# Attention in front of a two-layer feed-forward: exponentials and values of two batches as float16 pairs, and weight loads planned behind the splits of q and k

## The chip, the cores and the metric

The kernel runs on one core of a Trainium2 chip. The metric is the device time of one execution in microseconds. The engines are called TensorE (PE in the rows, its weight loads PEld), VectorE (DVE), ScalarE (ACT), GpSimd (POOL) and SyncE (SP, which issues nearly all DMAs).

## The reference

`q`, `k`, `v` have 4 batches, 12 heads, 448 positions and 64 columns a head. The output of attention, with its heads side by side, is the input of the feed-forward layers (768 to 2048 to 768).

```python
scores = scale * np.matmul(q, k.transpose(0, 1, 3, 2))
scores = cap * np.tanh(scores / cap)
scores = scores - np.max(scores, axis=-1, keepdims=True)
attn = np.exp(scores)
attn = attn / (np.sum(attn, axis=-1, keepdims=True) + 1e-09)
x = np.matmul(attn, v)                 # then heads side by side: (1792, 768)
h = x @ w_in
g = np.where(h >= 1, h, np.where(h <= -1, 0.0, (h + 1) ** 2 / 4))
out = g @ w_out
```

## The kernel before

**Numbers.** Float32 operands of the large products are split into two float16 halves ("high" and "low"), and a product is three float16 matmuls: high by high, high by low, low by high. This is so for q by k, x by `w_in` and g by `w_out`. The one large product left in float32 is exponentials by v (`av`).

**Attention.** It works on pairs of heads: `n` = 0 to 23, six to a batch (`NPR`). For each `n`, `split` makes the halves of q and k (`spl`); then for each of four chunks of keys `c` (the last one holds half a chunk of each head), `qk` writes scores into one of two PSUM tiles `s`, `expo` runs tanh and exp on ScalarE into `e` (a ring of five), `add` sums exponentials on VectorE, and `av` multiplies `e` by `v` into the one PSUM bank `av`. The two heads of `av` go to the two halves of the array's columns. `norm` sums over partitions (`t`), takes a reciprocal on VectorE, spreads it back over the partitions with a small matmul (`mix` by `sel`), scales, and splits the result into the halves `x`, of which a ring of ten is kept.

**Feed-forward.** For each batch `b`, `h_mm` makes 16 blocks of h (`f` = x by w, 18 matmuls each, lines L431 to L433; they need all six `x` of the batch), `h_out` makes the halves of g from them, and `o_mm` makes 6 blocks of the output (48 matmuls each, L460 to L462). During batch 0 the weights are loaded and converted piece by piece (`piece`: 16 pieces of `w_in`, 12 of `w_out`, lines L252 to L258); the pieces land in seven slots, the six tiles of `w2` and `raw`. Batches 1 to 3 load weights, then q, k and v again for range checks (`piece_check`, `qkv_check`), and `x_check` checks every `x`; `verdict` decides at the end whether a general version of the kernel has to run.

**Order.** Nothing is issued in the order in which it is written. Every step is recorded in a `Plan` with a cost per engine and its dependences by buffer names. `Plan.order` runs a list scheduler backwards and forwards five times and keeps the order with the earliest planned end. That order is then written out; each engine, and SP's queue of DMAs too, works through its own list in that order. Steps of attention of batch `b + 1` may be placed beside the feed-forward of batch `b`. A dependence that is only in the plan moves things in the lists; on the chip an instruction waits for real overlaps of tiles alone.

Of the kernel before, what the change touches and what calls it, by code (L numbers as in the profile page):

```python
# [32 lines left out]
CV, CX, CG = (CQ + i * B * NPR for i in (1, 2, 3))  # L33
NCHK = CG + B
# [5 lines left out]
WS, XS, GS, QS = 2.0 ** 15, 2.0 ** 13, 4.0, 2.0 ** 10  # L40
# [19 lines left out]
RATE = 250  # L60
# [5 lines left out]
class Plan:  # L66
# [4 lines left out]
    def __init__(self):  # L71
        self.steps, self.buffers = [], {}

    def add(self, options, reads=(), writes=(), size=0):

        i, deps = len(self.steps), set()
        for keys, write in ((reads, False), (writes, True)):
            for buf, part in keys:
                parts = self.buffers.setdefault(buf, {})
                for p in list(parts) if part is None else (part, None):  # L80
                    if p in parts:
                        deps.add(parts[p][0])
                        if write:
                            deps |= parts[p][1]
# [9 lines left out]
        self.steps.append(({e: (c, f) for e, c, f in options}, deps, size))  # L94
# [71 lines left out]
def fast_body(ctx, tc, flag, qkp, vp, cap, w_in, w_out, out):  # L166
# [25 lines left out]
    es = ring("e", 5, [P, 2, S])  # L192
    sums = ring("sums", 2, [P, 2, S])
    xs = ring("x", 10, [P, 2, S], F16)
# [6 lines left out]
    ots = ring("ot", 2, [P, S])  # L201
# [33 lines left out]
    def piece(i):  # L235
# [16 lines left out]
        dma(8 * P * width, lambda: M.dma_start(t, src.bitcast(I32)), [], rk)  # L252
# [18 lines left out]
    def x_check(n):  # L271
        x, k = st["x", n]
        j = CX + n
        dve(S, lambda: V.tensor_reduce(out=chk[:, j:j + 1], in_=x[:, 0], op=ALU.max, axis=AX.X, apply_absolute_value=True), [(k, 0)], [("chk", j)])
# [31 lines left out]
    def load_qk(n):  # L306
        t, k = st["qkr", n] = take("qkr", qkr)
        dma(4 * P * (S + KP), lambda: M.dma_start(t, qkp[n]), [], k)
# [4 lines left out]

    def split(n):

        (raw, rk), (t, k) = st["qkr", n], take("spl", spl)
        hk, lk = [(k[0][0], 0)], [(k[0][0], 1)]
        either(rk, hk, act_(S + KP, lambda: A.activation(t[:, 0], raw, AF.Copy, scale=QS)), dve_(S + KP, lambda: V.tensor_scalar(t[:, 0], raw, scalar1=QS, scalar2=None, op0=ALU.mult), True))
        dve(S + KP, lambda: V.scalar_tensor_tensor(out=t[:, 1], in0=raw, scalar=QS, in1=t[:, 0], op0=ALU.mult, op1=ALU.subtract), rk + hk, lk)
        st["spl", n] = t, hk + lk  # L320

    def qk(n, c):
# [10 lines left out]
        pe(640, run, k, sk)  # L333

    def expo(n, c):
        (s, sk), (e, ek) = st["s", n, c], take("e", es)
        st["e", n, c] = e, ek
        w = 2 if c < 3 else 1
        act(w * S + 60, lambda: A.activation(e[:, :w], s[:, :w, :S], AF.Tanh, scale=tsc), sk + [("tsc", None)], ek)  # L339
        act(w * S + 110, lambda: A.activation(e[:, :w], e[:, :w], AF.Exp, scale=capb), ek + [("tsc", None)], ek)  # L340
# [17 lines left out]
    def av(n, c):  # L358
        if c == 0:
            st["av", n] = take("av", avs)  # L360
        (a, ak), (vt, vk), (e, ek) = st["av", n], st["vt", n], st["e", n, c]

        def run():
            for j in range(2):
                h = slice(j * D, (j + 1) * D)
                w, m = (vt[:, j * 3 + c], e[:, j]) if c < 3 else (vt[h, 6], e[h, 0])
                T.matmul(a[h, :S], lhsT=w, rhs=m, start=(c == 0), stop=(c == 3))  # L367
        pe(790, run, ek + vk + (ak if c else []), ak)

    def norm(n):  # L370
# [16 lines left out]
        dve(1400, lambda: V.reciprocal(rr, t[:, :S // 2]), tk, rk)  # L387
# [15 lines left out]
        dve(S, lambda: V.scalar_tensor_tensor(out=xf, in0=xf, scalar=XS, in1=t[:, :S], op0=ALU.mult, op1=ALU.mult), tk + fk, fk)  # L403
# [3 lines left out]
    def attention(n):  # L407

        split(n)
        if n + 2 < B * NPR:  # L410
            load_qk(n + 2)
        for c in range(NCK):
# [3 lines left out]
            av(n, c)  # L416
# [53 lines left out]

    load_qk(0)
    dma(4 * P, lambda: M.dma_start(capr, cap.partition_broadcast(P)), [], [("tsc", None)])
# [11 lines left out]
    act(1, lambda: A.activation(half, ones[:, :1], AF.Copy, scale=0.5 * math.sqrt(GS)), [("ones", None)], [("half", None)])  # L484
    dve(1, lambda: V.reciprocal(tsc, capr), [("tsc", None)], [("tsc", None)])
# [13 lines left out]
    for b in range(B):  # L499
        for fc in range(NFC):  # L500
# [28 lines left out]
def general_body(ctx, tc, qkt, v, vf, cap, w_in, w_out, out):  # L529
# [421 lines left out]
    with tc.manual_schedule():  # L951
        for options, _, _ in plan.steps:
# [36 lines left out]
```

## Time and profile before

| | |
|---|---|
| Three runs, median | 651.07 us (650.08 to 651.25) |
| The profiled execution | 651.0 us, span 649.2 us |
| TensorE busy | 625.9 us, 96% of the span |
| VectorE busy | 449.2 us, 69% |
| ScalarE busy | 358.1 us, 55% |
| Mean granted TensorE clock | 0.987 |

The span runs from the first to the last instruction on the core, and 1.8 us of the execution lie around it. The busy share of TensorE is the union of its matmuls' durations; matmuls overlap, so what a stream of matmuls costs is read from the distance between their starts.

### The profile page before, as it was taken

To read this page: it belongs to the slowest core of one execution; us is meant where nothing else is said; L and a number is where in the kernel's file an instruction comes from. 1 tells how busy PE (TensorE), PEld (TensorE's weight loads), DVE (VectorE), ACT (ScalarE), POOL (GpSimd) and SP (SyncE) were. 2 spreads that over 40 slices of the span, in tenths; PEclk is the share of its full clock that TensorE was granted. 3 is DMA by queue.
4 is the path that set the end of the run, shared out by engine and by line. 5 is a ranking of instruction groups with operands and counts; after the bars stand their busy time and mean duration, and the time that the engine had idled before them with its cause. 6 is when DMAs were issued, how large, how long until landed. Compare 5 with 4: busy or idle time off the path is not lost.

```text
span 649.2 us, 8777 instructions
## 1 busy us (share of the span) xinstructions
PE 625.9 (96%) x3541; PEld 280.4 (43%) x3541; DVE 449.2 (69%) x610; ACT 358.1 (55%) x525; POOL 0.9 (0%) x5
## 2 busy tenths in 40 slices
PE   7599899999999999999999999999999999999996
PEld 2123245433355555333345554433345554555553
DVE  6989999999999235799962215999771226988400
ACT  6588986799941145999910026989830005552000
POOL 0000000000000000000000000000000000000000
PEclk9969999999999999999999999999999999999998
DMA  8935424534346012333544321332314445778401
GB/s 310 348 115 192 152 85 172 175 126 137 106 163 205 29 63 98 128 109 123 173 151 146 129 78 54 137 94 64 113 65 159 131 151 163 258 247 258 144 29 33
DMA packets 25538, 91.11 MB, mean 140 GB/s; under 512 B 2960, under 2 KB 12176, under 8 KB 22416
## 3 DMA queue, kind: packets, MB, share of 16 engines
q1 hardware_dynamic: 25488, 90.45, 41.6%
q8 instruction: 30, 0.49, 0.3%
q14 instruction: 20, 0.16, 0.1%
HBM read 84.94 MB, written 5.51 MB: 139 GB/s over the span
## 4 chain that ended last, share of the span: by engine, by line
PE 87%; ACT 9%; DVE 2%; DMA 1%; issue 1%; SPq 0%; ACTq 0%
PE f L460 11%; PE f L462 11%; PE f L461 11%; PE f L431 11%; PE f L433 11%; PE f L432 11%; PE av L367 10%; PE s L332 7%; ACT e L339 3%; ACT e L340 3%; PE t L381 2%; DMA capr<-cap 1%; PE t L398 1%; PE t L385 1%; ACT w L257 0%
## 5 line engine op out<-in xcount | busy, mean ns | idle before, releaser
L431 PE MATMUL f<-x,w 128*128 128x448 f16 x384 | 135.6, 353 | 0.9 <-ACT ot L467 0.7
L460 PE MATMUL f<-g,w 128*128 128x448 f16 x384 | 135.5, 353 | 0.0
L432 PE MATMUL f<-x,w 128*128 128x448 f16 x384 | 135.3, 352 | 0.0
L462 PE MATMUL f<-g,w 128*128 128x448 f16 x384 | 135.3, 352 | 0.0
L433 PE MATMUL f<-x,w 128*128 128x448 f16 x384 | 135.3, 352 | 0.0
L461 PE MATMUL f<-g,w 128*128 128x448 f16 x384 | 135.3, 352 | 0.0
L467 ACT ACTIVATE ot<-f 128x448 f32<-128x448 f32 x24 | 13.0, 543 | 164.7 <-PE f L462 164.7
L269 DVE TENSOR_REDUCE chk<-raw 128x1 f32<-128x768 f32 (+1 forms) x56 | 58.2, 1059 | 63.2 <-DMA raw<-w_out 63.2
L367 PE MATMUL av<-e,vt 128*64 128x448 f32 (+1 forms) x384 | 90.7, 565 | 3.3 <-ACT e L340 2.6
L340 ACT ACTIVATE e<-e,capb 128x896 f32<-128x896 f32 x96 | 91.0, 949 | 2.8
L339 ACT ACTIVATE e<-s,tsc 128x896 f32<-128x896 f32 x96 | 86.5, 902 | 9.0 <-PE s L332 5.8
L332 PE MATMUL s<-spl 64*128 64x448 f16 (+1 forms) x504 | 72.7, 368 | 7.2 <-ACT e L339 4.1
L443 ACT ACTIVATE r<-f,half 128x448 f32<-128x448 f32 x64 | 40.1, 627 | 44.1 <-PE f L433 43.9
L431 PEld LDWEIGHTS <-w 128*128 128x128 f16 x384 | 37.5, 98 | 42.3 <-issue 9.5
L445 DVE SCALAR_TENSOR_TENSOR wr<-f,r 128x448 f32<-128x448 f32 x64 | 39.5, 617 | 22.0 <-ACT r L444 21.5
L460 PEld LDWEIGHTS <-w 128*128 128x128 f16 x384 | 37.5, 98 | 39.1 <-issue 5.0
L433 PEld LDWEIGHTS <-w 128*128 128x128 f16 x384 | 37.6, 98 | 35.1
L462 PEld LDWEIGHTS <-w 128*128 128x128 f16 x384 | 37.6, 98 | 35.1
L461 PEld LDWEIGHTS <-w 128*128 128x128 f16 x384 | 37.6, 98 | 34.1
L432 PEld LDWEIGHTS <-w 128*128 128x128 f16 x384 | 37.6, 98 | 33.5 <-issue 1.4
L332 PEld LDWEIGHTS <-spl 64*128 64x128 f16 (+1 forms) x504 | 23.1, 97 | 64.0 <-issue 48.9
L448 ACT ACTIVATE g<-wr 128x448 f16<-128x448 f32 x59 | 33.8, 574 | 29.5 <-DVE wr L445 29.2
(64 smaller groups left out, 576.2 us busy)
## 6 DMA issues: line engine op xcount, KB each, us to landing
qkr<-qkp SPq DMA_DIRECT2D x48, 480.0 KB, 3.9
raw<-w_out SPq DMA_DIRECT2D x17, 1024.0 KB, 5.1
raw<-w_in SPq DMA_DIRECT2D x18, 768.0 KB, 4.2
w<-w_in SPq DMA_DIRECT2D x14, 768.0 KB, 8.7
vt<-vp SPq DMA_DIRECT2D x48, 224.0 KB, 3.4
w<-w_out SPq DMA_DIRECT2D x7, 1024.0 KB, 5.1
out<-ot SPq DMA_DIRECT2D x24, 224.0 KB, 2.0
capr<-cap SPq DMA_DIRECT2D x1, 0.5 KB, 6.4
```

Source lines behind the costliest of these rows:

```text
L269: dve(width, lambda j=j, op=op: V.tensor_reduce(out=chk[:, j:j + 1], in_=hi, op=op, axis=AX.X, apply_absolute_value=True), rk, [("chk", j)])
L332: T.matmul(s[:, j, :S], lhsT=t[h, a, S + c * P:S + (c + 1) * P], rhs=t[h, b, :S], start=(i == 0), stop=(i == 2))
L339: act(w * S + 60, lambda: A.activation(e[:, :w], s[:, :w, :S], AF.Tanh, scale=tsc), sk + [("tsc", None)], ek)
L340: act(w * S + 110, lambda: A.activation(e[:, :w], e[:, :w], AF.Exp, scale=capb), ek + [("tsc", None)], ek)
L367: T.matmul(a[h, :S], lhsT=w, rhs=m, start=(c == 0), stop=(c == 3))
L431: T.matmul(ph, lhsT=w1[:, 0, fc, c], rhs=x[c][0][:, 0], start=(c == 0), stop=False)
L432: T.matmul(ph, lhsT=w1[:, 1, fc, c], rhs=x[c][0][:, 0], start=False, stop=False)
L433: T.matmul(ph, lhsT=w1[:, 0, fc, c], rhs=x[c][0][:, 1], start=False, stop=(c == NCC - 1))
L443: act(S + (170 if acc else 0), lambda: A.activation(r, ph, AF.Relu, bias=half, scale=0.5 * root / (WS * XS), **acc), fk + [("half", None)] ...
L460: T.matmul(po, lhsT=hi[:, fc], rhs=gv[:, 0], start=(fc == 0), stop=False)
L461: T.matmul(po, lhsT=lo[:, fc], rhs=gv[:, 0], start=False, stop=False)
L462: T.matmul(po, lhsT=hi[:, fc], rhs=gv[:, 1], start=False, stop=(fc == NFC - 1))
```

## The change

- In batches 2 and 3 (`n >= HALVED`, 12 pairs of heads) exponentials and v are split into float16 halves (`halve`, `halve_v`), and `av` becomes three float16 products; exp gets a bias `lnes`, which scales it by 32. The reciprocals of these batches are checked (two reductions per `n` in `norm`).
- `av` of batches 1 to 3 is recorded for two chunks at once, so that its matmuls stand together in TensorE's list.
- `x_check` looks at one `x` of each batch (4 in all) where it looked at every one (24).
- The load of `cap` goes to ScalarE's queue as its first instruction; the first load of q and k is cut in two, and so is its split. In the plan, the first six weight pieces depend on the splits of q and k (`gate`).
- The planner counts DMAs at 400 bytes per ns (`RATE`, was 250), and steps of attention of batches 2 and 3 get a lead of 30 us in its priorities (`AHEAD`).
- Buffers: `x` has 7 tiles (10 before), `ot` one (2 before); halves of e use the two `z` tiles of the weight conversion and one more.

```diff
-RATE = 250
+RATE = 400
+
+AHEAD = 30000.0
...
-            out, _, end = self.run(deps, users, [-t for t in late], WINDOW, True)
+            out, _, end = self.run(deps, users, [-t - s[3] for t, s in zip(late, self.steps)], WINDOW, True)
...
+    ehs = [t.bitcast(F16)[:, :4 * S].rearrange("p (a j s) -> p a j s", a=2, j=2) for t in zs] + ring("eh", 1, [P, 2, 2, S], F16)
+    vhs = ring("vh", 2, [P, 2, TC, D], F16)
-    xs = ring("x", 10, [P, 2, S], F16)
+    xs = ring("x", 7, [P, 2, S], F16)
-    ots = ring("ot", 2, [P, S])
+    ots = ring("ot", 1, [P, S])
...
-        dma(8 * P * width, lambda: M.dma_start(t, src.bitcast(I32)), [], rk)
+        gate = [("gate", i)] if i < NPR else []
+        dma(8 * P * width, lambda: M.dma_start(t, src.bitcast(I32)), gate, rk)
...
+    def cuts(n):
+        return (slice(0, S + 2 * P), slice(S + 2 * P, S + KP)) if n == 0 else (slice(0, S + KP),)
...
+            dve(m, lambda w=w: V.scalar_tensor_tensor(out=t[:, 1, w], in0=raw[:, w], scalar=QS, in1=t[:, 0, w], op0=ALU.mult, op1=ALU.subtract), rz + hk, lk + [("gate", n)])
...
+    def halve(n, c):
+        (e, ek), w = st["e", n, c], 2 if c < 3 else 1
+        i = turn["eh"] = (turn.get("eh", -1) + 1) % len(ehs)
+        t, k = ehs[i], ehk[i]
+        hk, lk = [(k, 0)], [(k, 1)]
+        either(ek, [(k, None)], act_(w * S, lambda: A.copy(t[:, 0, :w], e[:, :w])), dve_(w * S, lambda: V.tensor_copy(t[:, 0, :w], e[:, :w]), True))
+        dve(w * S, lambda: V.tensor_tensor(out=t[:, 1, :w], in0=e[:, :w], in1=t[:, 0, :w], op=ALU.subtract), ek + [(k, None)], lk)
...
-    def av(n, c):
+    def av(n, cs):
+        if n >= HALVED:
+            vh, vk = st["vh", n]
+            def run():
+                for c in cs:
+                    e = st["eh", n, c][0]
+                    for x, y in ((0, 0), (0, 1), (1, 0)):
+                        for j in range(2):
+                            h = slice(j * D, (j + 1) * D)
+                            w, m = (vh[:, x, j * 3 + c], e[:, y, j]) if c < 3 else (vh[h, x, 6], e[h, y, 0])
+                            T.matmul(a[h, :S], lhsT=w, rhs=m, start=(c == x == y == 0), stop=(c == 3 and x == 1))
+            pe(105 + 570 * len(cs), run, [k for c in cs for k in st["eh", n, c][1]] + vk + (ak if cs[0] else []), ak)
+            return
...
+        if n >= HALVED:
+            for j, op in ((CS + n - HALVED, ALU.max), (CS + B * NPR + n - 2 * HALVED, ALU.min)):
+                dve(S // 2, lambda j=j, op=op: V.tensor_reduce(out=chk[:, j:j + 1], in_=rr, op=op, axis=AX.X), rk, [("chk", j)])
...
-            av(n, c)
+            if n >= HALVED:
+                halve(n, c)
+            if n < NPR:
+                av(n, [c])
+            elif c % 2:
+                av(n, [c - 1, c])
...
+    plan.add([("ACT", 50, lambda: A.dma_start(capr, cap.partition_broadcast(P)))], [], [("tsc", None)], 4 * P)
     load_qk(0)
-    dma(4 * P, lambda: M.dma_start(capr, cap.partition_broadcast(P)), [], [("tsc", None)])
...
-                for n in range(NPR):
-                    x_check(b * NPR + n)
+                x_check(b)
...
             for n in range(NPR):
+                plan.lead = AHEAD * (b > 0)
                 attention((b + 1) * NPR + n)
+                plan.lead = 0.0
```

The lists move in many places; three are shown. The first is SP's list at the start of the program, before: the loads of the first two pairs (`qkr`), of `cap`, of v (`vt`) and of weight pieces (`w2_0` to `w2_5`), up to the load of the third pair.

```order
L308 DMA qkr0_87<-qkp 128x960
L308 DMA qkr1_88<-qkp 128x960
L472 DMA capr_67<-cap 128x1
L252 DMA w2_0_78<-w_in 128x1536
L312 DMA vt0_91<-vp 128x448
L252 DMA w2_1_79<-w_in 128x1536
L312 DMA vt1_92<-vp 128x448
L252 DMA w2_2_80<-w_in 128x1536
L252 DMA w2_3_81<-w_in 128x1536
L252 DMA w2_4_82<-w_in 128x1536
L252 DMA w2_5_83<-w_in 128x1536
L308 DMA qkr0_87<-qkp 128x960
```

And the same list now:

```order
L322 DMA qkr0_87<-qkp 128x704
L322 DMA qkr0_87<-qkp 128x256
L322 DMA qkr1_88<-qkp 128x960
L326 DMA vt0_91<-vp 128x448
L326 DMA vt1_92<-vp 128x448
L264 DMA raw_84<-w_in 128x1536
L322 DMA qkr0_87<-qkp 128x960
L264 DMA w2_0_78<-w_in 128x1536
L322 DMA qkr1_88<-qkp 128x960
L264 DMA w2_1_79<-w_in 128x1536
```

The third pair's load stood behind six weight pieces and stands behind one now; the fourth stands behind two, and `cap` has left this list.

The second place is VectorE's list at the start of the program; before (`x9` is the zeroed tile that 13 warm-up matmuls of TensorE read, L481):

```order
L488 MEMSET sel_71 128x256
L483 MEMSET ones_70 128x32
L489 MEMSET low_72 128x1
L477 MEMSET x9_109 128x224
L493 MEMSET sel_71 2x64
```

And now (`x6` is that tile; the reciprocal reads `capr`, which the DMA of `cap` writes):

```order
L551 MEMSET sel_71 128x256
L547 MEMSET lnes_101 128x1
L545 MEMSET ones_70 128x32
L548 RECIPROCAL tsc_68<-capr_67 128x1
L552 MEMSET low_72 128x1
L539 MEMSET x6_110 128x224
L549 TENSOR_SCALAR tsc_68<-tsc_68 128x1
```

The reciprocal of `cap` stood ten rows behind the memset of that tile and stands two rows ahead of it now.

The third place is TensorE's list at the first chunk of `n` = 12, before (the float32 product of both heads is one row):

```order
L433 LDWEIGHTS w1_77
L433 MATMUL f0_139<-x8_108,w1_77 128x448
L367 MATMUL av0_141<-e3_96,vt0_91 64x448 x2
L332 LDWEIGHTS spl1_90
L332 MATMUL s0_137<-spl1_90 128x448
```

And now, with six such pairs of rows for each chunk (`z0` and `z1` hold the halves of e):

```order
L524 MATMUL f1_140<-g2_113,w2_5_83 128x448
L408 LDWEIGHTS vh0_99
L408 MATMUL av0_141<-z0_85,vh0_99 64x448
...
L408 LDWEIGHTS vh0_99
L408 MATMUL av0_141<-z1_86,vh0_99 64x448
L522 LDWEIGHTS w2_5_83
L522 MATMUL f1_140<-g3_114,w2_5_83 128x448
```

Two chunks now stand together between output blocks of batch 0 (L522 to L524); before, the first chunk stood alone among blocks of h of batch 1 (L433).

## Rows read from the trace of the kernel before

**Rows 1.** The page's first line.

```profile
span 649.2 us, 8777 instructions
```

**Rows 2.** Busy time of each engine by stretch, then granted clock, DMA share, GB/s.

```profile
20.00:30.00 10.00, 5.52 (x36) 1.78 (x36) 9.80 (x14) 5.20 (x10) 0.00 (x0) 1.00 0.87 339
30.00:40.00 10.00, 6.70 (x29) 2.27 (x31) 9.99 (x14) 6.81 (x9) 0.00 (x0) 0.55 0.78 241
...
120.00:180.00 60.00, 60.00 (x400) 21.68 (x399) 57.86 (x69) 57.64 (x81) 0.00 (x0) 1.00 0.47 157
...
325.00:400.00 75.00, 75.00 (x398) 38.58 (x397) 27.25 (x33) 13.10 (x25) 0.00 (x0) 1.00 0.36 120
```

**Rows 3.** Timeline of the start: start, duration, engine, instruction, idle time before it.

```profile
1.46 5.04 PE L481 MATMUL f<-x 128*128 128x448 f16 x13 [1.46 <-DVE x L477]
...
6.43 1.59 PE L332 MATMUL s<-spl 64*128 64x448 f16 x12
8.10 0.16 DVE L485 RECIPROCAL tsc<-capr 128x1 f32<-128x1 f32 x1 [1.50 <-DMA capr<-cap]
...
8.55 1.01 ACT L339 ACTIVATE e<-s,tsc 128x896 f32<-128x896 f32 x1 [1.70 <-DVE tsc L486]
...
13.10 1.08 DVE L348 TENSOR_TENSOR sums<-e,e 128x896 f32<-128x896 f32 x1
```

**Rows 4.** Timeline from the third pair's load to the last x of batch 0.

```profile
10.10 0.33 SPq L308 DMA_DIRECT2D qkr<-qkp  x1
...
30.09 0.65 DVE L318 TENSOR_SCALAR spl<-qkr 128x960 f16<-128x960 f32 x1
30.66 0.61 DVE L405 TENSOR_TENSOR x<-xf,x 128x448 f16<-128x448 f32 x1
...
33.36 1.01 ACT L339 ACTIVATE e<-s,tsc 128x896 f32<-128x896 f32 x1 [3.06 <-PE s L332]
...
77.49 0.48 PE L398 MATMUL t<-mix,sel 128*128 128x224 f32 x2 [0.49 <-DVE mix L394]
...
80.96 0.61 DVE L405 TENSOR_TENSOR x<-xf,x 128x448 f16<-128x448 f32 x1
```

**Rows 5.** Landing of the q and k loads, from the view of that tile.

```profile
DMA to landing us min/median/max: 3.0/3.9/12.3
```

**Rows 6.** The page's DMA issues: KB each, median us to landing.

```profile
out<-ot SPq DMA_DIRECT2D x24, 224.0 KB, 2.0
```

**Rows 7.** Groups by line: busy us, mean ns of one, then idle time before.

```profile
L340 ACT ACTIVATE e<-e,capb 128x896 f32<-128x896 f32 x96 | 91.0, 949 | 2.8
...
L339 ACT ACTIVATE e<-s,tsc 128x896 f32<-128x896 f32 x96 | 86.5, 902 | 9.0 <-PE s L332 5.8 <-DVE tsc L486 1.7 <-PE av L367 1.4
...
L387 DVE RECIPROCAL rr<-t 128x224 f32<-128x224 f32 x24 | 37.2, 1551 | 3.1 <-PE t L385 2.5 <-PE t L381 0.5
...
L367 PEld LDWEIGHTS av<-e,vt 128*64 128x64 f32 (+1 forms) x384 | 20.1, 135 | 42.7 <-issue 26.0 <-ACT e L340 8.6 <-ACT e L339 1.7
```

**Rows 8.** Timeline of TensorE in batch 2's attention.

```profile
266.91 0.35 PE L432 MATMUL f<-x,w 128*128 128x448 f16 x1
267.10 0.35 PE L433 MATMUL f<-x,w 128*128 128x448 f16 x1
267.38 0.97 PE L367 MATMUL av<-e,vt 128*64 128x448 f32 x4
268.29 1.31 PE L332 MATMUL s<-spl 64*128 64x448 f16 x12
269.53 0.36 PE L431 MATMUL f<-x,w 128*128 128x448 f16 x1
...
273.43 1.87 PE L367 MATMUL av<-e,vt 128*64 128x448 f32 x8
275.23 0.74 PE L332 MATMUL s<-spl 128*128 128x448 f16 x3
```

**Rows 9.** Timeline of TensorE at the end: its last matmul.

```profile
642.68 0.35 PE L462 MATMUL f<-g,w 128*128 128x448 f16 x1
```

More of the change, by code (lines that the diff above doesn't have):

```diff
@@ L32 @@
 CQ = 2 * NT
-CV, CX, CG = (CQ + i * B * NPR for i in (1, 2, 3))
-NCHK = CG + B
+CV, CX = (CQ + i * B * NPR for i in (1, 2))
+CG = CX + B
+CS = CG + B
+HALVED = 2 * NPR
+NCHK = CS + 2 * (B * NPR - HALVED)
 ADDED = 2 * NPR
@@ L71, in __init__ @@
     def __init__(self):
-        self.steps, self.buffers = [], {}
+        self.steps, self.buffers, self.lead = [], {}, 0.0
     def add(self, options, reads=(), writes=(), size=0):
@@ L93, in add @@
         deps.discard(i)
-        self.steps.append(({e: (c, f) for e, c, f in options}, deps, size))
+        self.steps.append(({e: (c, f) for e, c, f in options}, deps, size, self.lead))
     def run(self, before, after, prio, window, forward):
@@ L192, in fast_body @@
     es = ring("e", 5, [P, 2, S])
+    ehs = [t.bitcast(F16)[:, :4 * S].rearrange("p (a j s) -> p a j s", a=2, j=2) for t in zs] + ring("eh", 1, [P, 2, 2, S], F16)
+    ehk = ["z0", "z1", "eh0"]
+    vhs = ring("vh", 2, [P, 2, TC, D], F16)
+    lnes = new("lnes", [P, 1])
     sums = ring("sums", 2, [P, 2, S])
[L194 removed]
+    xs = ring("x", 7, [P, 2, S], F16)
     gsl = ring("g", NFC + 1, [P, S])
@@ L307, in load_qk @@
         t, k = st["qkr", n] = take("qkr", qkr)
-        dma(4 * P * (S + KP), lambda: M.dma_start(t, qkp[n]), [], k)
+        for z, w in enumerate(cuts(n)):
+            dma(4 * P * (w.stop - w.start), lambda w=w: M.dma_start(t[:, w], qkp[n][:, w]), [], [(k[0][0], z)] if n == 0 else k)
     def load_v(n):
@@ L312, in load_v @@
         dma(4 * P * TC * D, lambda: M.dma_start(t, vp[n]), [], k)
+    def cuts(n):
+        return (slice(0, S + 2 * P), slice(S + 2 * P, S + KP)) if n == 0 else (slice(0, S + KP),)
     def split(n):
         (raw, rk), (t, k) = st["qkr", n], take("spl", spl)
[L317 to L320, printed above, removed]
+        st["spl", n] = t, k[0][0]
+        for z, w in enumerate(cuts(n)):
+            rz, hk, lk, m = [(rk[0][0], z)], [(k[0][0], (z, 0))], [(k[0][0], (z, 1))], w.stop - w.start
+            either(rz, hk, act_(m, lambda w=w: A.activation(t[:, 0, w], raw[:, w], AF.Copy, scale=QS)), dve_(m, lambda w=w: V.tensor_scalar(t[:, 0, w], raw[:, w], scalar1=QS, scalar2=None, op0=ALU.mult), True))
+            dve(m, lambda w=w: V.scalar_tensor_tensor(out=t[:, 1, w], in0=raw[:, w], scalar=QS, in1=t[:, 0, w], op0=ALU.mult, op1=ALU.subtract), rz + hk, lk + [("gate", n)])
     def qk(n, c):
@@ L332, in run @@
                     T.matmul(s[:, j, :S], lhsT=t[h, a, S + c * P:S + (c + 1) * P], rhs=t[h, b, :S], start=(i == 0), stop=(i == 2))
-        pe(640, run, k, sk)
+        pe(640, run, [(k, (z, i)) for z in range(len(cuts(n)) if c > 1 else 1) for i in range(2)], sk)
     def expo(n, c):
@@ L356, in add @@
                 dve(S, lambda h=h, j=j: V.tensor_tensor(out=t[h, j], in0=t[h, j], in1=e[h, 0], op=ALU.add), ek + tk, tk)
-    def av(n, c):
-        if c == 0:
+    def av(n, cs):
+        if cs[0] == 0:
             st["av", n] = take("av", avs)
-        (a, ak), (vt, vk), (e, ek) = st["av", n], st["vt", n], st["e", n, c]
-        def run():
[L364 to L368, printed above, removed]
+        (a, ak), (vt, vk) = st["av", n], st["vt", n]
+        if n >= HALVED:
[10 more added lines that the diff above has]
+            return
+        def run():
+            for c in cs:
+                e = st["e", n, c][0]
+                for j in range(2):
+                    h = slice(j * D, (j + 1) * D)
+                    w, m = (vt[:, j * 3 + c], e[:, j]) if c < 3 else (vt[h, 6], e[h, 0])
+                    T.matmul(a[h, :S], lhsT=w, rhs=m, start=(c == 0), stop=(c == 3))
+        pe(105 + 800 * len(cs), run, [k for c in cs for k in st["e", n, c][1]] + vk + (ak if cs[0] else []), ak)
     def norm(n):
@@ L386, in norm @@
         pe(500 if last is None else 900, run, mk + lk + [("ones", None)], tk)
-        dve(1400, lambda: V.reciprocal(rr, t[:, :S // 2]), tk, rk)
+        dve(1340, lambda: V.reciprocal(rr, t[:, :S // 2]), tk, rk)
         act(S, lambda: A.copy(xf, a[:, :S]), ak, fk)
@@ L484, in fast_body @@
     act(1, lambda: A.activation(half, ones[:, :1], AF.Copy, scale=0.5 * math.sqrt(GS)), [("ones", None)], [("half", None)])
+    dve(1, lambda: V.memset(lnes, math.log(ES)), [], [("tsc", 0)])
     dve(1, lambda: V.reciprocal(tsc, capr), [("tsc", None)], [("tsc", None)])
@@ L951, in general_body @@
     with tc.manual_schedule():
-        for options, _, _ in plan.steps:
+        for options, *_ in plan.steps:
             next(iter(options.values()))[1]()
```

30 lines of the change are left out of this document (20 added, 10 removed).

## The prediction

> **What bounds the kernel now.** I read the stretches first. From 90 us to 640 us TensorE has no idle time worth naming: 60.00 of 60 us between 120 and 180 us, 75.00 of 75 between 325 and 400 [rows 2]. In the first 85 us it waits: 5.52 us busy of 10 between 20 and 30 us, and right behind that the granted clock is 0.55 for ten microseconds, so most of them at the lower of its two levels (1.2 GHz), after the idle stretch [rows 2]. So the time has three parts: a start, up to the last half of `x` of batch 0, from which the stream of h blocks can flow; TensorE's work behind it; and a tail. In the trace the start ends at 81.57 us (80.96 + 0.61, the sixth row of that kind) [rows 4], the last matmul starts at 642.68 us [rows 9], and the tail to 649.2 us [rows 1] is 6.5 us. The profiled execution took 651.0 us, 1.8 us more than its span and the median of the runs within 0.1 us; I add those 1.8 us.
>
> What TensorE's work costs is read from starts [rows 8]: h and output blocks 0.19 us a matmul (266.91 to 267.10), a block to an `av` group 0.28 us instead, one chunk of float32 `av` 0.91 us (267.38 to 268.29), two in a row 1.80 us (273.43 to 275.23), six rounds of half-array float16 scores 1.24 us (268.29 to 269.53). Priced so, and counted from the lists, all matmuls of before make 618.0 us. From the last small spread matmul of batch 0 (77.49 us [rows 4]) to the end they make 563.5 us, and the trace has 642.68 − 77.49 = 565.2 us there: prices and counts hold to 0.3%.
>
> **The change, part by part.**
>
> *`av` in halves.* 48 chunks lose 0.903 us each (43.3 us) and gain three rounds of two matmuls. The nearest row is the score group: float16, 448 columns, two half-array matmuls side by side, 1.24 us for six rounds [rows 8]. I take 1.24 us for two chunks: 24 × (1.80 − 1.24) = 13.4 us less. The unknown is whether a round of column halves runs as tightly as one of row halves. Lower bound: 0.57 us a chunk, as taken. The float32 rows show column halves running side by side: four matmuls of two passes each (0.37 us a matmul) fit in 0.90 us where one after the other would need 1.49, but 0.15 us of that is more than streaming, 0.08 a round. With 0.08 in each float16 round a chunk costs 0.80 us, and the gain falls by 11 us. Upper bound: every load in full, 0.135 us [rows 7] on 0.19 a round, 0.97 us a chunk, 19 us worse than taken.
>
> Here a rule speaks against the change. Between the starts of two h matmuls, 0.19 us apart, lies a weight load for the same rows of the array, and it costs nothing visible. The Trainium skill, TensorE: Matmul & The Clock Gate, Part 3 ("The mechanism"), says that a weight load overlaps with matmuls in flight only when the row groups differ; both heads of `av` use all rows. By that rule every load would be exposed and the whole gain on TensorE gone; by the rows it stays. I go by the rows, and keep the exposed load as a rival.
>
> *Groups.* The lists have 278 changes between kinds of matmul where they had 259; each costs 0.09 us (0.28 against 0.19 [rows 8]): +1.7 us. All matmuls of the new list make 605.8 us, 552.6 us of them behind the end of the start. (3.2 us of batch 1's attention, which TensorE did ahead of that point, now lie behind it.)
>
> *The start.* The third pair's load is issued at 10.10 us [rows 4] and takes up to 12.3 us to land [rows 5], behind six weight pieces; its split stands further back in VectorE's list and runs at 30.09 us, and ScalarE meets its first tanh of that pair at 33.36 us, after 3.06 us of idling for it [rows 4]; between 20 and 30 us ScalarE works 5.20 us of 10, VectorE 9.80 [rows 2]. So the hole is first the DMA queue's and then VectorE's, which converts weights while the pair waits. In the new list the third pair's load stands behind one weight piece, and its split comes ahead of all conversions; the gates themselves are no waits on the chip, only places in the lists. The first conversions will not starve: the second piece has 4.7 MB up to its end where the third pair's load had 6.0 MB and was there by 22.4 us (10.10 + 12.3), so some 18 us by proportion, and VectorE reaches it at about 17. From the first sum to the last `x` half VectorE had 81 instructions, 35 of them conversions and 3 checks; it has 67 now, 20 of them conversions and no check. Their prices are the page's durations less 0.08 us, because each starts that much before the one ahead of it ends (30.09 + 0.65 against 30.66 [rows 4]): 12 sums at 1.00 [rows 3], 6 reciprocals at 1.47 [rows 7], 4 low halves of q and k at 1.07, conversions 13.8 together, the rest 11.5; sum 50.4 us. Before it was 63.4 us by the same prices, spread over 68.5 us (13.10 to 81.57 [rows 3, 4]). ScalarE needs 50.1 us there, 44 of them tanh and exp (24 × 0.902 + 24 × 0.949 [rows 7]), TensorE 48: VectorE still sets the pace, and 3 us of waits are my estimate (it was 5).
>
> The first exponential does not come earlier, against what the new place of `cap` suggests. The reciprocal, which waits for `cap`, now stands ahead of the memset that the warm-up needs. Before, warm-up ran at 1.46 us for 5.04 us and scores from 6.43 us [rows 3], under cover of the loads. `cap` on ScalarE's queue lands at best 2.0 us after its issue at about 0.7 (as the output tiles do [rows 6]), at worst about as now, just ahead of 8.10 us [rows 3]. I take 3.0: the tile is alone on its queue. Warm-up then starts at 3.5, scores at 8.5, the first tanh at 9.6 (8.55 before [rows 3]), the first sum 4.5 us later, as before, at 14.1. The cut load of the first pair is hidden by this. So the start ends at 14.1 + 50.4 + 3 = 67.5 us; with `cap` at its bounds 67 to 72.
>
> *New work elsewhere.* VectorE gets 48 low halves of e (36 × 1.00, 12 × 0.53), 12 of v (0.53) and 24 reductions (0.3), some 56 us, and loses 20 checks at 0.53; ScalarE gets about 40 us of casts. What hides this are the stretches of output blocks, such as 325 to 400 us, where VectorE works 27.25 us of 75 and ScalarE 13.10 [rows 2]; the planner's lead draws batch 2's and 3's attention into them. On the path this costs nothing by itself. Late next is the conversion of `w_out`: batch 1's attention now lies wholly behind the start, beside it. From the end of the start to the last weight piece VectorE's list holds 146 us, and TensorE has 149 us of work until it needs that piece; before, the same sum left 8.5 us. Between 120 and 180 us VectorE worked 57.86 us of 60 [rows 2], 3.6% lost to waits; 3.6% of 146 is 5 us, against a slack of 3. With the shorter tight spots (0.5 us over, at four h blocks) I put 4 us of new waits of TensorE, between 0 and 9.
>
> *Sum.* 67.5 + 552.6 + 6.5 + 1.8 + 4 = 632.4; I say 632 us, 19 less than now: 14.1 from the start and 13.4 from `av`, less 1.7 for changes between kinds, 3.2 for work moved behind the start, 4 for new waits.
>
> **The rivals.**
>
> A. Loads show in the float16 rounds. For it: the 0.08 us in the float32 rounds, which gives 0.80 us a chunk and 643 us. Against: the score groups, float16 like the new ones, show nothing of it. Chance 0.11. With loads exposed in full, 0.97 us a chunk, the time is 651 us; no group in the trace looks like that, so 0.03. (This is what the rule of the Trainium skill named above, TensorE: Matmul & The Clock Gate, Part 3, would make of the time.)
>
> B. The start gains little, because VectorE, ScalarE and TensorE are all within 5 us of full there, or because `cap` lands late and the clock falls again: end of the start at 76 us or later, 641. Chance 0.12.
>
> C. VectorE falls behind in batch 0's second half by more than I allow, 10 to 14 us instead of 4: 638 to 642. Chance 0.08.
>
> D. Slower: the two heads' matmuls run one after the other. A chunk is then 6 × 0.19 = 1.13 us, 27 us worse: 659. It decides from 0.97 us a chunk on (19 us over 48 chunks). Against it speaks the float32 group. Chance 0.03.
>
> E. Everything fits: no new waits, start over by 62 us: 623. Chance 0.04.
>
> **How the numbers follow.** The forecast has 0.59. Its own range is 625 to 640 (start ± 4, new waits 0 to 9). A measurement here tells 0.2%, 1.3 us, from no change. A range of 621 to 646 takes in B, C, E and A up to 0.86 us a chunk; D and the far end of A stay out, about 0.1. Slower: D and a sliver of A, 0.04; within 0.2%: the end of A, 0.03; faster 0.93.
>
> **What the profile would show.** The sixth `x` half near 67 us; no ten-microsecond stretch of the start at the lower clock; the warm-up starting behind `cap`, near 3.5 us; groups of 12 float16 `av` matmuls followed 1.24 us later by the next kind; TensorE's idle time behind the start under 9 us, most of it before 215 us and put down to VectorE's conversions. Wrong I would be if those groups take 1.5 us and more, if the start ends after 72 us, or if TensorE waits in batches 2 and 3 for halves of e, which the sums of work do not show.

## The result and the profile after

The changed kernel takes 639.98 us (median of 4 runs, 639.36 to 641.26) against 650.58 us (4 runs of the kernel before on the same chip): a ratio of 0.9842, 95% interval 0.9825 to 0.9859, or 10.6 us less. The forecast was 632 us, in a range of 621 to 646. The page of the changed kernel begins:

```profile
span 638.4 us, 9097 instructions
...
PE 613.3 (96%) x3637; PEld 281.9 (44%) x3637; DVE 495.5 (78%) x687; ACT 397.3 (62%) x579; POOL 0.9 (0%) x5
```

Stretches of it, with the columns of [rows 2]:

```profile
20.00:30.00 10.00, 9.78 (x81) 2.85 (x77) 9.62 (x12) 9.50 (x13) 0.00 (x0) 1.00 0.49 171
30.00:40.00 10.00, 9.32 (x64) 2.80 (x64) 9.50 (x14) 9.84 (x13) 0.00 (x0) 1.00 0.91 327
60.00:70.00 10.00, 7.54 (x42) 2.86 (x42) 10.00 (x16) 3.96 (x9) 0.00 (x0) 0.83 0.44 150
70.00:80.00 10.00, 8.22 (x44) 4.16 (x43) 9.74 (x15) 6.48 (x11) 0.00 (x0) 1.00 0.48 157
120.00:180.00 60.00, 58.40 (x379) 23.18 (x378) 58.00 (x70) 54.57 (x77) 0.00 (x0) 1.00 0.43 136
325.00:400.00 75.00, 75.00 (x443) 35.43 (x438) 49.55 (x63) 37.64 (x55) 0.00 (x0) 1.00 0.42 143
```

The hole of 20 to 40 us [rows 2] is gone. A smaller one is new at 60 to 80 us, with VectorE full, and TensorE is no longer without gaps between 120 and 180 us. The timeline of the start answers to [rows 3, 4]:

```profile
0.72 0.40 ACTq L533 DMA_DIRECT2D capr<-cap  x1
5.67 0.17 DVE L548 RECIPROCAL tsc<-capr 128x1 f32<-128x1 f32 x1 [4.50 <-DMA capr<-cap]
6.14 5.00 PE L543 MATMUL f<-x 128*128 128x448 f16 x13 [6.14 <-DVE tsc L549]
11.07 1.31 PE L351 MATMUL s<-spl 64*128 64x448 f16 x12
11.85 1.01 ACT L358 ACTIVATE e<-s,tsc 128x896 f32<-128x896 f32 x1 [3.78 <-PE s L351]
...
67.50 0.62 DVE L460 TENSOR_TENSOR x<-xf,x 128x448 f16<-128x448 f32 x1
```

The sixth low half of `x` ends at 68.12 us, 13.4 us earlier than before. And TensorE's rows there, where it waits for VectorE (`mix` is what the spread matmul reads, `wr` is the instruction that empties an `f` bank):

```profile
65.30 0.54 PE L449 MATMUL t<-mix,sel 128*128 128x224 f32 x2 [2.46 <-DVE mix L445]
72.65 0.35 PE L493 MATMUL f<-x,w 128*128 128x448 f16 x1 [1.78 <-DVE wr L507]
```

**One account for all runs.** The sixth low half turned out a poor mark for the end of the start, so I use another: the work that TensorE's matmuls up to a time t make at the prediction's prices [rows 8] (changes between kinds at 0.28 us, the small products at their least distance), and what t exceeds it by, TensorE's loss up to t. Its totals of work lie 13 to 14 us below the prediction's 618.0 and 605.8, so only differences between rows are read. Work and losses are those of the profiled execution, which took up to 1.9 us more (E3) or 1.5 us less (E6) than the median in the second column. Work, loss up to 80 us, and loss from there to the last matmul, in us:

| Kernel | Time | Work | Loss to 80 | Loss behind |
|---|---|---|---|---|
| before | 650.6 | 603.6 | 31.2 | 8.0 |
| changed | 640.0 | 592.4 | 23.6 | 16.1 |
| no gate, cap and cut undone (E1) | 634.4 | 591.4 | 20.2 | 14.2 |
| no gate (E2) | 637.4 | 592.0 | 21.6 | 16.8 |
| cap undone (E3) | 639.4 | 592.6 | 22.2 | 18.1 |
| warm-up first (E4) | 639.5 | 592.4 | 22.2 | 16.7 |
| E1 at rate 250 (E5) | 643.6 | 592.8 | 29.0 | 13.0 |
| changed at rate 250 (E6) | 643.4 | 591.9 | 23.1 | 18.4 |
| no halves (E7) | 647.8 | 604.5 | 24.3 | 10.0 |
| gate alone (E12) | 639.5 | 592.5 | 21.9 | 16.4 |

So the change takes 11.2 us of work and 7.6 us of early loss away, and gives 8.1 us back behind 80 us; 1.8 of the 8.1 are `av` groups that took longer than their price. Priced by the usual distances between starts in these traces instead, the three are 9.3, 7.2 and 5.9 us.

### The profile page after: what moved, and what is told of

Its sections match the earlier page's. It is cut to its first block, busy times and chain, and to the rows that moved or that the text cites. A ratio compares the mean times of both kernels' runs of the same rounds, so it can differ in the third digit from the quotient of the medians.

```text
span 638.4 us, 9097 instructions
## 1 busy us (share of the span) xinstructions
PE 613.3 (96%) x3637; PEld 281.9 (44%) x3637; DVE 495.5 (78%) x687; ACT 397.3 (62%) x579; POOL 0.9 (0%) x5
## 4 chain that ended last, share of the span: by engine, by line
PE 64%; ACT 22%; DVE 7%; DMA 4%; issue 2%; ACTq 0%
PE f L522 12%; PE f L524 11%; PE f L523 11%; ACT e L360 7%; ACT e L358 7%; PE f L493 6%; PE f L495 6%; PE f L494 6%; PE av L408 4%; PE s L351 4%; DMA qkr<-qkp 4%; PE av L418 2%; DVE chk L295 2%; ACT r L505 2%; ACT r L506 2%
## 5 line engine op out<-in xcount | busy, mean ns | idle before, releaser
L522 PE MATMUL f<-g,w 128*128 128x448 f16 x384 | 135.6, 353 | 0.0
L524 PE MATMUL f<-g,w 128*128 128x448 f16 x384 | 135.3, 352 | 0.0
L358 ACT ACTIVATE e<-s,tsc 128x896 f32<-128x896 f32 x96 | 86.4, 901 | 14.4 <-PE s L351 14.2
L351 PE MATMUL s<-spl 64*128 64x448 f16 (+1 forms) x504 | 68.7, 352 | 1.2 <-ACT e L358 1.0
L522 PEld LDWEIGHTS <-w 128*128 128x128 f16 x384 | 37.5, 98 | 41.4 <-issue 8.7
L524 PEld LDWEIGHTS <-w 128*128 128x128 f16 x384 | 37.6, 98 | 35.0
L360 ACT ACTIVATE e<-e,lnes,capb 128x896 f32<-128x896 f32 (+1 forms) x48 | 49.8, 1039 | 1.1
L360 ACT ACTIVATE e<-e,capb 128x896 f32<-128x896 f32 (+1 forms) x48 | 45.6, 949 | 1.4
L418 PE MATMUL av<-e,vt 128*64 128x448 f32 (+1 forms) x192 | 44.2, 559 | 1.9 <-ACT e L360 1.2
```

The source lines that it names most:

```text
L351: T.matmul(s[:, j, :S], lhsT=t[h, a, S + c * P:S + (c + 1) * P], rhs=t[h, b, :S], start=(i == 0), stop=(i == 2))
L522: T.matmul(po, lhsT=hi[:, fc], rhs=gv[:, 0], start=(fc == 0), stop=False)
L524: T.matmul(po, lhsT=hi[:, fc], rhs=gv[:, 1], start=False, stop=(fc == NFC - 1))
```

## The experiments

Times are medians beside 9 to 11 runs of the kernel before on the same chip (650.7 to 651.3 us).

**E1, the start as it was.**

```diff
-        gate = [("gate", i)] if i < NPR else []
+        gate = []
...
-        return (slice(0, S + 2 * P), slice(S + 2 * P, S + KP)) if n == 0 else (slice(0, S + KP),)
+        return (slice(0, S + KP),)
...
-    plan.add([("ACT", 50, lambda: A.dma_start(capr, cap.partition_broadcast(P)))], [], [("tsc", None)], 4 * P)
     load_qk(0)
+    dma(4 * P, lambda: M.dma_start(capr, cap.partition_broadcast(P)), [], [("tsc", None)])
```

> The changed kernel with the three edits to its start undone: the weight loads wait for nothing, cap goes second in SP's queue, and the first pair's q and k come in one load and one split. The planner's new rate and lead and the halves of batches 2 and 3 stay. In SP's queue five weight pieces then stand ahead of the third pair's q and k, where the changed kernel has one. Theory (the start gains because the third pair's load and split no longer wait behind weight loads and conversions): the third pair's split starts at 25 to 30 us, ScalarE idles again between 20 and 30 us, the sixth low half of x ends at 75 to 80 us in place of 68.1, and the time is 647 to 652 us. Rival (the new rate moves the loads by itself, and the gate is idle): sixth low half by 70 us, time 639 to 643 us. Rival (the work put off is made up for elsewhere, so that an early start is lost later): sixth low half at 75 us or later, but time under 645 us.

634.44 us (634.05 to 636.32), ratio 0.9746 [0.9728, 0.9763]: 5.5 us faster than the changed kernel (6.2 by their ratios to the kernel before on either chip), which none of the three had said. The third pair's split starts at 20.38 us, the sixth low half ends at 69.57 us, ScalarE has no hole. The first theory falls: the gate did not make the start's gain, and a later sixth half went with an earlier end. Where the difference arises is seen in VectorE's timeline, first of the changed kernel:

```profile
8.34 1.15 DVE L339 SCALAR_TENSOR_TENSOR spl<-qkr,spl 128x960 f16<-128x960 f32 x1
15.67 0.66 DVE L338 TENSOR_SCALAR spl<-qkr 128x960 f16<-128x960 f32 x1 [6.18 <-PE s L351]
16.25 1.09 DVE L384 TENSOR_TENSOR sums<-e,e 128x896 f32<-128x896 f32 x1
...
19.32 1.03 DVE L265 TENSOR_SCALAR z<-w 128x768 int32<-128x768 int32 x2
```

and of E1:

```profile
11.03 0.56 DVE L265 TENSOR_SCALAR z<-w 128x768 int32<-128x768 int32 x1 [0.88 <-DMA w<-w_in]
11.63 0.96 DVE L266 SCALAR_TENSOR_TENSOR z<-w,z 128x768 int32<-128x768 int32 x1
12.62 0.96 DVE L267 SCALAR_TENSOR_TENSOR z<-w,z 128x768 int32<-128x768 int32 x1
```

With the gate the third pair's split stands ahead of all conversions in VectorE's list; it waits for the first pair's scores, which read the tile that it writes (there are two), and everything behind it waits along: 6.18 us. E1 converts weights there. By 20 us VectorE has finished 9 of the instructions that convert weights there, the changed kernel one. The stretches show no later idle time of VectorE in which this could be made up; the changed kernel, then E1:

```profile
0.00:20.00 20.00, 12.35 (x62) 4.03 (x62) 8.29 (x28) 11.29 (x13) 0.19 (x4) 1.00 0.71 244
20.00:80.00 60.00, 54.83 (x360) 19.51 (x357) 58.62 (x80) 48.90 (x68) 0.00 (x0) 0.97 0.54 186
80.00:200.00 120.00, 118.39 (x720) 50.98 (x718) 117.83 (x144) 97.69 (x137) 0.00 (x0) 1.00 0.49 161
```

```profile
0.00:20.00 20.00, 15.76 (x88) 4.82 (x88) 12.85 (x32) 14.34 (x17) 0.19 (x4) 1.00 0.85 319
20.00:80.00 60.00, 54.53 (x358) 19.33 (x357) 58.45 (x78) 55.46 (x77) 0.00 (x0) 1.00 0.53 187
80.00:200.00 120.00, 117.59 (x724) 51.86 (x722) 117.68 (x144) 96.36 (x135) 0.00 (x0) 1.00 0.47 158
```

From 20 to 200 us VectorE (third pair of columns) is 98% busy in both; in the first 20 us it has 4.6 us less with the gate. The last conversion starts at 218.32 us there and at 214.07 us here:

```profile
218.32 1.21 DVE L270 SCALAR_TENSOR_TENSOR w<-z,w 128x1024 f16<-128x1024 f32 x1
```

```profile
214.07 1.23 DVE L270 SCALAR_TENSOR_TENSOR w<-z,w 128x1024 f16<-128x1024 f32 x1
```

**E2, the gate's line alone undone; E12, gate alone** (cap and cut undone).

> The changed kernel with only the waits of the first weight loads taken out; cap and the cut first pair stay as changed. Four weight pieces stand in SP's queue ahead of the third pair's q and k, where the changed kernel has one. Theory (it is the gate that gives the start): the third pair's split starts at 22 to 26 us, sixth low half of x at 72 to 76 us, time 643 to 648 us. Rival (cap, the cut pair and the rate give it): sixth low half by 69.5 us, time 638.5 to 641.5 us.

> The changed kernel with cap back in SP's queue and the first pair in one piece, but with the gate: with 634.4 us without all three edits, 637.4 with cap and cut alone and 640.0 with all, this is the fourth corner. Theory (gate and early cap each hold back VectorE's first conversions): VectorE busy 8 to 11 of the first 20 us, sixth low half of x at 64 to 68 us, time 636 to 639.5 us. Rival (cap and cut do the harm, the gate none): time 633.5 to 635.5 us. Rival (the gate does all of it): time 639.5 to 642 us.

E2: 637.44 us (636.37 to 638.81), split at 22.49 us, sixth half at 71.11 us. Both lines fail: the half is 3 us later than the changed kernel's and the time 2.5 us shorter. E12: 639.51 us (639.0 to 642.9), on the line between the theory and the rival that the gate does all; VectorE busy 9.21 us of the first 20, sixth half at 66.59 us. With E1 and the changed kernel these are four corners: 634.4 with none, +3.0 for cap and cut, +5.1 for the gate, +5.5 for all. The gate alone accounts for nearly all of the harm, and the two don't add up. In E12 the third pair's split again stands ahead of the conversions, and VectorE waits 3.91 us there, this time for that pair's load. Where the gate's price comes back is seen between 60 and 80 us, in E1, then in E12, and in E12's two longest waits there (us in total, times, longest):

```profile
60.00:80.00 20.00, 18.07 (x109) 7.22 (x110) 19.61 (x27) 17.06 (x27) 0.00 (x0) 1.00 0.51 169
```

```profile
60.00:80.00 20.00, 14.41 (x79) 6.85 (x72) 19.74 (x29) 10.41 (x19) 0.00 (x0) 1.00 0.42 132
```

```profile
PE t L449 <- DVE mix L445: 2.5, 1, 2.5
PE f L493 <- DVE wr L507: 2.4, 1, 2.4
```

TensorE is busy for 3.7 us less there, which is most of the 5.1. The other kernels agree: 14.4 to 15.8 us of these 20 in the seven kernels with the gate (changed, E3, E4, E6, E7, E8, E12), each with a wait of 1.8 to 2.5 us for `wr`, and 18.0 to 20.0 in the five without (E1, E2, E5, E9, E10), none of them with a wait for `wr` there.

**E3, cap back on SP's queue; E4, the warm-up's tile cleared first.** E3 moves cap's load as in E1; E4's edit:

```diff
+    first = len(plan.steps)
...
+        order = list(plan.order())
+        order.sort(key=lambda step: step[0] != first)
```

> The changed kernel with cap's load back in SP's queue, second, behind the first piece of q and k; all else as changed. In the changed kernel cap went first on ScalarE's queue and took 4.9 us to land, so that the reciprocal that waits for it started at 5.67. Theory (cap is on the path of the start only up to the first tanh at 11.85, and VectorE sets the start's end): the reciprocal starts at 4 to 6.5 us, the sixth low half of x ends at 67 to 70 us, time 638.5 to 642 us. Rival (cap's early load is what the start needs): first tanh 2 us later than 11.85 or more, time 642 us or more.

> The changed kernel with one instruction moved: VectorE clears the tile of the warm-up first, before the reciprocal that waits for cap, so that the warm-up no longer waits for cap. The order is otherwise the same on every engine. Theory (in the changed kernel the warm-up starts at 6.14 behind cap and holds up the first scores until 11.07, and this is on the start's chain): warm-up at 1.5 us, scores at 7 to 8.5, first tanh at 8 to 9.5, first sum at 12.5 to 14, sixth low half of x at 65 to 66.5, time 636.5 to 638.5 us. Rival (VectorE's 50 us of work set the start's end whatever the first tanh): first tanh as above, but sixth low half at 67.5 or later, time 639 to 641 us.

E3: 639.40 us (638.85 to 641.25); E4: 639.47 us (637.3 to 640.22). In both, the first tanh starts 3 us earlier (8.93 and 8.58 us), the sixth low half ends at 65.3 us, 2.8 us before the changed kernel's, and the time is the same within 0.6 us. E4's lists are the changed kernel's but for that one instruction: its first conversion starts 2.2 us earlier and its last one 1.1 us earlier (217.22 us), so even of the time that VectorE gains, half is gone by then. E4's theory falls with that, and its rival too, since the half did move. E4's rows behind the start say where the gain went:

```profile
62.45 0.48 PE L449 MATMUL t<-mix,sel 128*128 128x224 f32 x2 [2.46 <-DVE mix L445]
...
69.80 0.35 PE L493 MATMUL f<-x,w 128*128 128x448 f16 x1 [2.43 <-DVE wr L507]
```

TensorE fills its two `f` banks with h blocks and waits for VectorE to empty them (`wr`), which stands behind five conversions in its list. The earlier start lengthens that wait, from 1.78 to 2.43 us. Late cap, the warm-up behind it and the cut are worth nothing here while the gate stands.

**E5 and E6, the planner's rate.** In both `RATE = 400` becomes 250; E5 on top of E1, E6 on the changed kernel.

> As the kernel without the three edits to the start (634.4 us), and the planner's rate back at 250 as well; its lead for the last three batches and the halves stay. The third pair's q and k then stand behind six weight pieces in SP's queue, as in the kernel before, and its split behind the first pair's x on VectorE. Theory (it is the planner's rate, and not the gate, that brought the third pair forward): third pair's split at 28 to 34 us, ScalarE idle for 3 us or more between 20 and 40 us, sixth low half of x at 75 to 83 us, time 641 to 648 us. Rival (some other edit that is still in, the lead or the rings, gives the start): sixth low half by 72 us, time 633 to 637 us.

> The changed kernel with the planner's rate back at 250; gate, early cap and cut first pair stay. One weight piece stands ahead of the third pair's q and k. Theory (gate and rate do the same to the start, and the gate's price is that the weights are converted late, so that TensorE waits between 60 and 80 us and behind): third pair's split at 15 to 18 us, sixth low half of x at 66 to 70 us, time 637 to 644 us. Rival (the gate needs the rate): sixth low half at 73 us or later, time 645 us or more. Rival (a rate of 250 serves the later stages better than 400): time under 636 us.

E5: 643.55 us (643.28 to 643.98); split at 30.59 us, the sixth half at 81.20 us, the hole is back. So the rate made the start's gain: 9.1 us from E5 to E1, without any gate. With gate, cap and cut it is worth 3.4 us (E6 to the changed kernel). E6: 643.36 us, split at 17.71 us, sixth half at 67.39 us. Both theories hold. At rate 250 gate, cap and cut move the half by 13.8 us and the time by 0.2 us: 5.9 us less loss up to 80 us, 5.4 us more behind. It was not mainly the load that the rate brought forward: the third pair's is issued at 8.23 us in E1 and at 8.62 in E5, and lands at 19.73 and 21.61 us. It is the split's place: with the rate at 400 it stands nine rows further ahead in ScalarE's list and starts 10.2 us earlier, E1 first, then E5:

```profile
20.38 0.99 ACT L338 ACTIVATE spl<-qkr 128x960 f16<-128x960 f32 x1
```

```profile
30.59 1.00 ACT L338 ACTIVATE spl<-qkr 128x960 f16<-128x960 f32 x1
```

The prediction said "the hole is first the DMA queue's and then VectorE's". In the kernel before, that load lands at 21.82 us and the split starts 8.3 us behind it; in E1 a load that lands at 19.73 us leaves no hole. So the queue sets when the split can start at the earliest, and most of the hole is the lists'. The gate does bring the load's landing forward, to 12.46 us in the changed kernel, but that isn't where the time is.

**E7, no halves** (`HALVED = B * NPR`, and no range checks of halved batches).

> The changed kernel with no batch in halves: the exponentials and v of the last two batches go through TensorE as in the first two, with no splits and no checks of them; all else as changed. Theory (halving takes 11 us of TensorE's work off the span, and TensorE sets the end in batches 2 and 3): time 647 to 652 us, and between 320 and 480 us TensorE waits less than 2 us. Rival (VectorE's 46 us of added work takes back most of what the halves give): time 639 to 645 us.

647.77 us (646.39 to 649.18): the halves are worth 7.8 us. The account says why not 12: 12.1 us of work, less 6.1 us more loss behind 80 us, of which 1.8 are the price of the `av` groups and 4.3 are waits. The theory holds, its time at the lower end, and TensorE has no wait of 0.12 us or more between 320 and 480 us: the halves save TensorE's work, and waits take about a third of it back. By the lists of waits TensorE waits 9.5 us for VectorE in the changed kernel and 6.4 in E7 (the warm-up's wait left out).

**E8, the heads' loop turned round.**

```diff
-                    for x, y in ((0, 0), (0, 1), (1, 0)):
-                        for j in range(2):
+                    for j in range(2):
+                        for x, y in ((0, 0), (0, 1), (1, 0)):
```

> The changed kernel with one loop turned round: in the last two batches the three products of one head come in a row, where they alternated between the two heads, which use different halves of TensorE's columns. Same matmuls, same operands. Theory (the two heads' matmuls run side by side only because they alternate): a group of 12 that takes 1.31 us now takes 2.2 to 2.6 us, and 24 groups make the time 660 to 670 us. Rival (matmuls on different column halves are overlapped in any order, or the loads of weights set the pace): a group at 1.3 to 1.5 us, time 638 to 645 us.

640.98 us (640.16 to 641.6). The rival holds; two full chunks of E8 take 1.26 us, as they do in the changed kernel, which is shown first:

```profile
221.72 1.33 PE L408 MATMUL av<-z,vh 128*64 128x448 f16 x12
222.98 0.36 PE L522 MATMUL f<-g,w 128*128 128x448 f16 x1
```

```profile
221.84 1.33 PE L408 MATMUL av<-z,vh 128*64 128x448 f16 x12
223.10 0.36 PE L522 MATMUL f<-g,w 128*128 128x448 f16 x1
```

Over 24 groups the distance to the next kind is 1.316 us in the changed kernel (0.28 of it the change of kind) and 1.326 in E8. Twelve matmuls at 0.19 us each would take 2.27 us one after the other, so they run two at a time even when the three of one head are issued in a row; which two run together, the rows don't tell.

**E9, VectorE held** by 22 fills of a tile ahead of E1's first conversion.

> The kernel without the three edits to the start (634.4 us), with VectorE kept busy for 4.4 to 5.3 us more ahead of its first weight conversion at 11 us, by 22 fills of a tile that nothing reads. In the runs so far VectorE is busy 8.29 of the first 20 us with the gate and 12.85 without it, and about 98 percent from 20 to 200 us in both. Theory (VectorE has no slack up to 200 us, so that the 4.6 us for which the gate leaves it idle come back as waits of TensorE): time 637.5 to 641 us, with TensorE's waits spread over 60 to 200 us. Rival (VectorE's queue has slack, and the gate costs by the order in which things are done): time 633 to 636 us.

642.34 us (641.42 to 643.14). The fills took 8.13 us where 4.4 to 5.3 were meant, and the time lies above the theory's range; a row of VectorE's timeline, and one of TensorE's:

```profile
10.22 8.13 DVE L593 MEMSET idle<- 128x240 f32 x22
```

```profile
24.62 0.98 PE L432 MATMUL t<-sums,ones 128*32 128x224 f32 x8 [7.08 <-DVE sums L387]
```

The first conversion starts 7.2 us later (18.27 against 11.03 us) and the kernel ends 7.9 us later: the rival falls. But the wait is not spread, as expected, it comes at once, since the fills hold up the first sums as well. So E9 shows what it costs to hold all of VectorE's work in the start; what late conversions alone cost it does not show, and E4 shows that it can be less than their delay.

**E10, no lead** (E1 with `AHEAD = 0`).

> The kernel without the three edits to the start (634.4 us), and with the planner's lead for the last batches at 0; rate 400 and the halves stay. Theory (the rate alone makes the gain at the start, the lead is worth little): third pair's split at 19 to 24 us, sixth low half of x at 68 to 73 us, time 633 to 638 us. Rival (the lead keeps attention of the last batches from being late): time 639 us or more, with TensorE waiting for exponentials or their halves between 200 and 480 us.

671.95 us (668.43 to 673.64): 37.5 us worse, so the rival holds, by far more than its bound. The start's gain needs no lead, though: the split starts at 20.36 us, as the theory has it, and the sixth half ends at 66.10, earlier still. TensorE waits for nothing between 60 and 80 us here, so an early half alone does not make the wait for `wr`. Two stretches behind the start:

```profile
200.00:260.00 60.00, 60.00 (x329) 30.40 (x329) 33.88 (x47) 30.22 (x48) 0.00 (x0) 1.00 0.31 107
260.00:325.00 65.00, 52.85 (x353) 21.74 (x350) 60.14 (x81) 62.11 (x86) 0.00 (x0) 0.89 0.22 67
```

VectorE and ScalarE work half of the time up to 260 us and are full behind it, while TensorE waits. Of the waits from 200 to 480 us, 6.9 us are for `mix`, 4.6 for tanh that empties a tile of scores, and 0.5 for halves. The lead spreads the new work over both stretches.

**E11, three batches in halves** (E1 with `HALVED = NPR`).

> The kernel without the three edits to the start (634.4 us), with three batches in halves in place of two: the second batch too goes through TensorE as float16 pairs. That takes about 6 us of TensorE's work away and puts about 23 us more on VectorE and ScalarE, most of it between 80 and 240 us, where VectorE has about 2 us of slack up to 200 and 4 to 8 us from 200 to 260. Theory (there VectorE sets the pace): time 638 to 652 us. Rival (TensorE sets the pace there as well): time 626 to 632 us.

669.73 us: 35 us worse than E1, where 4 to 18 were expected. The execution that was profiled took 1593 us against 668.3 to 669.9 of the five others, with matmuls of 0.76 us where 0.35 is usual, so its times are not used, and where the 35 us arise stays open. Its lists tell of a rival that the theory left out: halves of `e` and weight conversions share the two `z` tiles, and here the halves of the second batch meet the conversions. In VectorE's list 93 rows, 23 of them low halves of `e`, stand between the 68th and the 69th of its 116 rows of conversion; in E1 the longest such stretch is 13 rows. No run tests it.

## Why the prediction held in its range and missed its point

**The start's end: right in size by luck, and the wrong mark.** 67.5 us was forecast for the sixth low half, 68.12 measured, because two errors cancelled: cap was taken at 3.0 us and landed in about 4.9 (the reciprocal that waits for it started at 5.67), the warm-up started at 6.14 in place of 3.5, the first sum at 16.25 in place of 14.1, and VectorE then needed 51.9 us in place of 53.4. The step that failed is the one ahead of it, "a start, up to the last half of `x` of batch 0, from which the stream of h blocks can flow". The stream did not flow: TensorE waited for `mix` and `wr` and ran for some microseconds at the lower clock (0.83 from 60 to 70 us), all behind VectorE's list. The half came 13.4 us earlier and the loss up to 80 us fell by 7.6. E3, E4 and E6 move the half without the time, E1 the time without the half.

**"The first conversions will not starve."** This failed too. VectorE's list put the third pair's split ahead of them, the prediction took that for gain alone, and it cost 6.18 us of an engine that is 98% busy from 20 to 200 us. "The gates themselves are no waits on the chip, only places in the lists" was right, and the place is what cost: 5.1 us from E1 to E12, 3.7 of them between 60 and 80 us, where TensorE waits for VectorE. The prediction credited the new list; that the rate had made it, and the gate added nothing, only E1 and E5 show.

**`av` in halves: right.** 13.4 us was the term; at 1.316 us for two chunks, where 1.24 was taken, it is 11.6. The rule of the Trainium skill (TensorE: Matmul & The Clock Gate, Part 3, "The mechanism": a weight load overlaps with matmuls in flight only where the row groups differ) would have made it no gain; both heads use all 128 rows, and the loads stay hidden. Of rivals A and D nothing is seen, in E8 neither.

**New waits: mis-sized, and half misplaced.** 4 us were put for them. Behind the sixth half TensorE took 564.0 us to its last matmul (632.09) where 552.6 + 4 were summed, 7.4 us more: 1.8 for the `av` groups, and the rest, 5.6, on the 4, so nearly 10 us of waits, which is rival C's size, if not its place alone. With 0.6 us from the start's end this makes up the 8 us between forecast and measurement. From 66 us on the gaps of more than 0.12 us beyond price sum to 12.8 us: 5.8 up to 162 us, 1.6 between 217 and 317, 2.7 between 405 and 466, 2.6 between 548 and 571. "Most of it before 215 us" was wrong. The last are VectorE's checks of batch 3, which wait for their loads while `wr` stands behind them:

```profile
569.26 1.15 DVE L295 TENSOR_REDUCE chk<-qkr 128x1 f32<-128x960 f32 x1 [0.98 <-DMA qkr<-qkp]
570.33 0.62 DVE L507 SCALAR_TENSOR_TENSOR wr<-f,r 128x448 f32<-128x448 f32 x1
...
571.00 0.35 PE L493 MATMUL f<-x,w 128*128 128x448 f16 x1 [1.21 <-DVE wr L507]
```

That the halves' 56 us of VectorE's work cost nothing on the path does not fit E7 (4.3 us of waits), though by VectorE's other work coming late and not by TensorE waiting for halves: no such wait is in the changed kernel's list of waits.

```profile
PE f L493 <- DVE wr L507: 5.6, 4, 1.8
PE t L449 <- DVE mix L445: 3.0, 2, 2.5
```

**What made the 10.6 us.** By the runs: halves, lead and the other edits together 7.1 us (before to E5), the rate 9.1 (E5 to E1), less 5.5 for gate, cap and cut, taken in this order; in another the rate is worth 3.4 and the gate nothing (E6). The kernel of E1 beats both, 16.8 us under the kernel before on its chip.

## What to carry to other kernels

When two engines are nearly full, follow the second one's whole queue and not the one event that the first waits for: moving an instruction that must itself wait to the head of a full engine's list costs that engine the wait. Check a planned order by the idle time of the engine that has no slack later on, even in a stretch where nobody waits for it. And when a change edits a planner's constants beside its rules, price them apart: here, without the gate, the rate was worth 9 us and the lead, with halves and rate in, 37; the gate on top of them cost 5.

## What the runs showed of the hardware that was not expected

- Exponentials with a bias tile take 1039 ns in place of 949 (mean of the same two shapes). In E7, where none has a bias, all of 128x896 take 1041 ns; with a bias they take 1132 in the changed kernel:

```profile
L360 ACT ACTIVATE e<-e,lnes,capb 128x896 f32<-128x896 f32 (+1 forms) x48 | 49.8, 1039 | 1.1
...
L360 ACT ACTIVATE e<-e,capb 128x896 f32<-128x896 f32 (+1 forms) x48 | 45.6, 949 | 1.4
```

- A load of 0.5 KB that was alone on ScalarE's queue, issued at 0.72 us, released its reader at 5.67 us; on SP's queue behind one load it started at 4.82 us in E3, behind the first piece of the first pair, and at 6.62 in E1, behind all of it.
- Fills of one tile in a row (E9) started 0.37 us apart, where each lasts 0.26 us by the profile:

```profile
L593 DVE MEMSET idle<- x22: 258/258/258, 10.2 to 18.1; 128x240 f32 x22
```
